# Decay attention and four experts on one core: the own terms of units 2 and 3 from a t-major product summed on VectorE

## The chip, the core and the metric

The kernel runs on one core of a Trainium2 chip. The metric is the device time of one execution in microseconds; the time before is the median of three runs, 913.03 us (912.9 to 913.32). Beside it stands one profiled execution, from which all durations below are read.

## The reference

Two parts follow each other. The first is a recurrence with a decaying state, for 4 batches, 8 heads, 768 steps and 48 dimensions per head; the second sends its output, as 3072 rows of 384 numbers, through 4 experts and weights them with `domain_probs`.

```python
for t in range(S):
    kt, vt, rt, wt = (k[:, :, t], v[:, :, t], r[:, :, t], w[:, :, t])
    cur = np.einsum('bhd,bhe->bhde', u[None] * kt, vt)
    y[:, :, t] = np.einsum('bhd,bhde->bhe', rt, state + cur)
    state = wt[:, :, :, None] * state + np.einsum('bhd,bhe->bhde', kt, vt)
...
p = domain_probs / (domain_probs.sum(-1, keepdims=True) + 1e-09)
for e in range(E):
    h = np.maximum(x @ w1[e], 0.0)
    out += p[:, e:e + 1] * (h @ w2[e])
```

The term with `cur` is what a step gives to itself: for each head it is the number `sum over d of r*u*k` times v. These numbers are called own terms here.

## The kernel before

The 768 steps are cut into 6 chunks of 128; a chunk of one batch is a unit, and there are 24: unit n is batch n % 4 of chunk n // 4. Units 0 to 3 are the first chunk. A unit goes through these helpers, all nested in `chunked_path`:

- `load` (L164) issues its transfers on SyncE's queue: `w` (tile wx), `k`, `r` with the head's dimension on the partitions (d-major), `v` with the step on the partitions (t-major), and `own`: r and k t-major in one tile `rkt` of 128x768, from a pool with one buffer.
- `after_decays` and `until_decays` (L237 to L259) make the products of decays on VectorE: the scan L241 to tile g, two tiny steps L251 and L252, the scan L253 to tile e. `scale` (L261) multiplies r by e (L263) and k by g (L264), in place, on VectorE.
- `own_product` and `diag_sum` (L184, L208) make the own terms, 8 per step, in tile dg (128x8). For chunk 0 POOL (VectorE for unit 0) multiplies r and k d-major (L192, 112x512), TensorE multiplies that with u in four products of 2 columns each (L215), and ScalarE copies the sums out of PSUM (L216). For all later chunks POOL multiplies r and k t-major and then u, which stands repeated in tile u_sb (L194, L195, 128x384 each), and VectorE sums over the dimensions (L218).
- `place` (L220) spreads dg over an identity, one half of the heads per call, to tile a0 or a1: either in four scaled copies on ScalarE (L227) or in one multiplication on POOL (L229). `DIAG` says which; for units 2 and 3 it is POOL for a0 and ScalarE for a1.
- `scores` (L266): TensorE multiplies scaled k and r (L272) and transposes k (L278). `masking` (L285) writes the scores below the diagonal into a0 and a1 on VectorE (L288). `values` (L290) multiplies a0 and a1 with v (L302, L306; ScalarE copies the result out, L308) and `carry` (L359) updates the state (L368).
- `guard` (L376) is a test of the decays on ScalarE (L379, L380).

The experts work on the output of a chunk. `f1` (L397) makes one of 8 slices of the hidden layer: TensorE (L405 for the first expert on chunk 0, otherwise L411), then ScalarE's relu to tile hh (L417) and VectorE's remainder to tile hl (L418); the product stands in one of three PSUM buffers, pf1, until both have read it. `f2` (L420) is the second layer (L431). The weights arrive as tiles `raw` and are split by `split_w` (L146) in two parts, with a cast on ScalarE (L151) and two subtractions on POOL (L156).

Everything is issued in an order written by hand from L558 on, and each engine works through its instructions in that order. While units 1 to 3 are made, the first expert's slices for batch 0 and batch 1 go in between: `begin(b, f)` is slice f for batch b, and `split_w2(q)` splits quarter q of the first expert's w2. A list `steps` holds the helpers of the units from unit 2's scores on; `go()` takes the next from it. For unit n they are `step_a` (after_decays of n+1, scores of n, own_product of n+1), `step_b` (until_decays of n+1), `step_c` (masking of n), `step_d` (scale, diag_sum and place of n+1, then the transfer `own` of unit n+2) and `step_e` (values and carry of n, and transfers). So unit 3's scale, diag_sum and place stand in `step_d(2)`, ahead of begin(1,5), and unit 2's values follow it.

```python
            begin(1, f)
            if f in (0, 1, 3, 4, 5):
                go()
            if f == 2:
                split_w2(2)
                guard(1)
                load(4, "w")
```

Of the kernel before, what the change touches and what calls it, by code (L numbers as in the profile page):

```python
# [39 lines left out]
SEG = (2, 2)  # L40
# [6 lines left out]
def chunked_path(ctx, tc, dmaj, tmaj, u_bc, probs, w1, w2, out, flag):  # L47
    nc = tc.nc
# [25 lines left out]
    u_sb = const.tile([128, DM], F32, name="u_sb")  # L74
# [20 lines left out]
    def setup_a():  # L95
        nc.gpsimd.memset(zero.bitcast(F32), 0.0)
        nc.gpsimd.memset(u_col, 0.0)
        nc.vector.memset(ones1, 0.0)
        nc.vector.memset(ones1[:, C + 1::C + 1], 1.0)
        nc.vector.memset(zst, 0.0)  # L100
        nc.gpsimd.memset(ident, 1.0)
        nc.gpsimd.affine_select(out=ident, in_=ident, compare_op=ALU.is_gt, fill=0.0, base=0,
                                pattern=[[1, C]], channel_multiplier=-1)
        nc.gpsimd.tensor_copy(mask, ident)
        make_identity(nc, ident)

    def act_table():
        nc.vector.memset(chk[:, 0:1], 0.0)
        nc.scalar.copy(chk[:, 1:2], chk[:, 0:1])
# [26 lines left out]
    def load_own(q):  # L136
        nc.sync.dma_start(out=w1_own[:, q], in_=w1[0, q])
# [26 lines left out]
    def load(n, what):  # L164
        if n >= NU:
            return
        s = un.setdefault(n, dict(c=n // B, b=n % B))
        if what == "w":
            s["wx"] = p_wx.tile([ROWS, WLEN], F32, name="wx", tag="wx")
            nc.sync.dma_start(out=s["wx"], in_=dmaj[n, :, 2 * NP * C:])  # L170
        elif what in ("r", "k"):
            x = p_in.tile([ROWS, NP, C], F32, name=what, tag=what)
            o = 0 if what == "r" else NP * C
            nc.sync.dma_start(out=x, in_=dmaj[n, :, o:o + NP * C].rearrange("p (i t) -> p i t", i=NP))
            s[2 * what] = x
        elif what == "own":
            t = p_one.tile([128, 2 * DM], F32, name="rkt", tag="rkt")
            nc.sync.dma_start(out=t, in_=tmaj[n, :, 0:2 * DM])
            s["rt"], s["kt"] = t[:, 0:DM], t[:, DM:2 * DM]
        else:  # L180
            s["v"] = p_in.tile([128, DM], F32, name="v", tag="v")
            nc.sync.dma_start(out=s["v"], in_=tmaj[n, :, 2 * DM:])

    def own_product(n):  # L184
        s = un[n]
        if s["c"] == 0:

            if not spare:
                spare.append(p_acc.tile([128, B, DM], F32, name="acc", tag="acc").rearrange("p b d -> p (b d)"))
            o = n % 2 * NP * C  # L190
            t = s["own"] = spare[0][0:ROWS, o:o + NP * C].rearrange("p (i t) -> p i t", i=NP)
            (nc.vector if n == 0 else nc.gpsimd).tensor_tensor(t, s["rr"], s["kk"], ALU.mult)  # L192
            return
        nc.gpsimd.tensor_tensor(s["rt"], s["rt"], s["kt"], ALU.mult)  # L194
        nc.gpsimd.tensor_tensor(s["rt"], s["rt"], u_sb, ALU.mult)  # L195

    def load_u():
        for j in range(2):
            nc.sync.dma_start(out=u_col[half(j), :, j],
                              in_=u_bc[0, :].rearrange("(i j d) -> j d i", j=2, d=D)[j],  # L200
                              allow_slow_non_contiguous=True)
# [6 lines left out]
    def diag_sum(n):  # L208
        s = un[n]
        dg = s["dg"] = p_two.tile([128, 2, NP], F32, name="dg", tag="dg")  # L210
        s["a"] = []
        if s["c"] == 0:
            p = ps_f2.tile([128, DM], F32, name="pf2", tag="pf2")[:, 0:2 * NP].rearrange("p (j i) -> p j i", j=2)
            for i in range(NP):
                nc.tensor.matmul(p[:, :, i], s["own"][:, i, :], u_col[:, i, :], start=True, stop=True)  # L215
            nc.scalar.copy(dg, p)  # L216
        else:
            nc.vector.tensor_reduce(dg, s["rt"].rearrange("p (i j d) -> p j i d", j=2, d=D), AX.X, ALU.add)  # L218
# [339 lines left out]
    with tc.manual_schedule():  # L558
        act_table()
        setup_a()  # L560
        for what in ("w", "k", "r"):
            load(0, what)
        load_u()
        load(0, "v")
        warm_up(FILL[0])
        for what in ("w", "k", "r"):
            load(1, what)
        load_own(0)
        load(1, "v")
        load_own(1)  # L570
        load(2, "w")
        load_own(2)
        setup_b()


        after_decays(0)
        own_product(0)
        own_score(0)
        until_decays(0)
        warm_up(FILL[1])  # L580
        scale(0)
        last_pair(0)
        own_product(1)
        after_decays(1)
        scores(0)
        for what in ("k", "r"):
            load(2, what)
        load_own(3)
        for q in range(2):
            more_raw()  # L590
        masking(0)
        last_pair(1)
        until_decays(1)
        values(0)
        diag_sum(1)
        carry(0)
        load(2, "v")
        place(1, 0)
        scale(1)

        def begin(b, f):
            f1(passes[0][1], 0, f, b * C, C, True)

        def split_w2(q):
            split_next((passes[0][1], 2, q), True)

        begin(0, 0)
        scores(1)
        for what in ("k", "r"):
            load(3, what)  # L610
        for q in range(2):
            more_raw()
        place(1, 1)
        after_decays(2)
        own_product(2)
        begin(0, 1)
        masking(1)
        begin(0, 2)
        guard(0)
        load(3, "w")  # L620
        split_w2(0)
        values(1)
        carry(1)
        load(3, "v")
        begin(0, 3)
        until_decays(2)
        begin(0, 4)
        begin(0, 5)
        scale(2)
        last_pair(2)  # L630
        diag_sum(2)
        begin(0, 6)
        split_w2(1)
        place(2, 0)
        place(2, 1)
        begin(0, 7)
        nc.sync.dma_start(out=u_sb, in_=u_bc)
        nc.sync.dma_start(out=pr, in_=probs)
        del steps[-2 * len(parts):]
        for f in range(FT):  # L640
# [7 lines that stand above are left out]
            if f == 4:  # L648
                last_pair(3)
            if f == 6:  # L650
                split_w2(3)
        script = {7: (go,), 8: (go,), 9: (setup_c, lambda: guard(2), lambda: load(5, "w"), go),
                  10: (go, lambda: guard(3), lambda: split_x(0)), 12: (lambda: split_x(1),), 13: (go,)}
        for pi, (g, e) in enumerate(passes):
            first, last = pi % NE == 0, pi % NE == NE - 1
            for blk in g:
                segs = SEG if pi == 0 else (B,)
                b0 = 0
                for nb in segs:
                    next_w1 = blk == g[-1] and pi + 1 in fresh and b0 + nb == B  # L660
                    own_w2 = blk == g[0] and pi in fresh and pi > 0
                    if pi == 0:
                        pace[:] = 0.2, 0.6
                    elif blk >= GROUPS[-1][0]:
                        pace[:] = 0.6, 1.0
                    else:
                        pace[:] = 0.4, 0.8

                    def work(i):
                        q = i % FT // 2  # L670
                        if own_w2 and i < FT and i % 2 == 0:
                            split_next((e, 2, q), True)
                        if next_w1 and i >= FT and i % 2 == 0:
                            split_next((passes[pi + 1][1], 1, q), True)
                        if i == FT - 1 and last and b0 + nb == B:
                            read.add(blk)
                        if pi == 0 and b0 == 0:
                            for f in script.get(i, ()):
                                f()
                            return True  # L680
                        if pi == 0 and i in (9, 11):
                            split_x(2 + (i - 9) // 2)

                    if first:
                        upto(blk * B + b0 + nb - 1)
                    turn(e, blk, first, last, b0, nb, pi == 0, pi == 0 and b0 == 0, work)
                    b0 += nb
# [189 lines left out]
```

## Time and profile before

| what | value |
|---|---|
| median of three runs | 913.03 us |
| the profiled execution | 913.18 us |
| its span, first to last instruction | 911.5 us |
| TensorE busy | 899.6 us, 99% |
| VectorE busy | 351.5 us, 39% |
| ScalarE busy | 257.8 us, 28% |
| POOL busy | 267.1 us, 29% |
| read from memory | 60.86 MB |

The execution's own time is longer than the span by what lies before the first and after the last instruction. PE is TensorE, DVE VectorE, ACT ScalarE, POOL GpSimd, and SP SyncE, which issues the transfers. An engine's busy time is a sum over the whole span; where it waits, and for whom, is told by the views that go by time.

### The profile page before, as it was taken

The page shows a single profiled execution, that of the slowest core. Times are in us where ns is not written, and L with a number is a line of the kernel's source. Part 1 is how long each engine was busy: PE and PEld are TensorE (multiplying, and loading weights), DVE is VectorE, ACT ScalarE, POOL GpSimd, SP SyncE. Part 2 cuts the span into 40 slices and gives each one's busy share as a digit, 9 for nine tenths or more (in the row PEclk, how much of TensorE's full clock was granted, in tenths as well). Part 3 has the DMA queues.
Part 4 walks back from the last instruction along what each step waited for, and adds up shares of the span by engine and source line. Part 5 has one row for each costly group of instructions (what it writes and reads, how often), then busy time and mean ns, then how long its engine had stood idle before and what let it go on. Part 6 is the DMA issues. An engine that isn't in the chain of part 4 may idle for free.

```text
span 911.5 us, 13796 instructions
## 1 busy us (share of the span) xinstructions
PE 899.6 (99%) x5675; PEld 810.2 (89%) x5675; DVE 351.5 (39%) x564; ACT 257.8 (28%) x482; POOL 267.1 (29%) x278
## 2 busy tenths in 40 slices
PE   8999999999999999999999999999999999999997
PEld 6898989898898988998989889899899899889987
DVE  6756555546363622122455642202222221221221
ACT  4555343322234132133221332232212310321110
POOL 3638766622255332033312220042003300230000
PEclk9999999999999999999999999999999999999999
DMA  9625435441334222111324210021002200110001
GB/s 249 196 65 180 158 119 170 137 129 56 93 105 147 67 70 68 35 58 65 105 72 131 75 49 29 1 79 61 1 1 70 69 1 1 35 35 36 18 18 38
DMA packets 36423, 70.48 MB, mean 77 GB/s; under 512 B 5376, under 2 KB 15488, under 8 KB 36352
## 3 DMA queue, kind: packets, MB, share of 16 engines
q1 hardware_dynamic: 36352, 69.53, 24.7%
q8 instruction: 46, 0.75, 0.4%
q14 instruction: 25, 0.20, 0.1%
HBM read 60.86 MB, written 4.72 MB: 72 GB/s over the span
## 4 chain that ended last, share of the span: by engine, by line
PE 98%; ACT 1%; DVE 1%; issue 0%; POOL 0%; DVEq 0%; ACTq 0%; POOLq 0%
PE pf L431 44%; PE pf L411 41%; PE sc L272 3%; PE yp L322 2%; PE pf L405 2%; PE yp L317 1%; PE kt L278 1%; PE up L368 1%; PE pf L115 1%; ACT a L227 0%; PE pf L215 0%; PE pf L302 0%; PE pf L306 0%; DVE zst L251 0%; ACT wx L380 0%; DVE a L288 0%
## 5 line engine op out<-in xcount | busy, mean ns | idle before, releaser
L411 PE MATMUL pf<-x,w1h 128*128 128x512 f32 x1104 | 342.0, 391 | 0.0
L431 PE MATMUL pf<-w2h,hh 128*128 128x384 f32 x768 | 259.7, 338 | 0.0
L431 PE MATMUL pf<-w2h,hl 128*128 128x384 f32 x768 | 257.2, 335 | 0.0
L431 PE MATMUL pf<-w2l,hh 128*128 128x384 f32 x768 | 256.9, 335 | 0.0
L418 DVE SCALAR_TENSOR_TENSOR hl<-pf,hh 128x512 fp32r<-128x512 f32 (+2 forms) x208 | 134.7, 649 | 285.0 <-ACT hh L417 284.3
L411 PEld LDWEIGHTS pf<-x,w1h 128*128 128x128 f32 x1104 | 205.8, 188 | 42.4 <-issue 0.4
L417 ACT ACTIVATE hh<-pf 128x512 fp32r<-128x512 f32 (+2 forms) x208 | 117.2, 565 | 428.1 <-PE pf L411 417.0
L411 PE MATMUL pf<-x,w1l 128*128 128x512 f32 x552 | 215.2, 390 | 0.0
L156 POOL TENSOR_TENSOR w1l<-raw,w1h 128x384 fp32r<-128x384 f32 x72 | 74.8, 1068 | 253.0 <-ACT w1h L151 253.0
L431 PEld LDWEIGHTS pf<-w2h,hh 128*128 128x128 f32 x768 | 144.2, 188 | 2.2 <-issue 0.4
L431 PEld LDWEIGHTS pf<-w2l,hh 128*128 128x128 f32 x768 | 144.2, 188 | 0.9
L431 PEld LDWEIGHTS pf<-w2h,hl 128*128 128x128 f32 x768 | 144.1, 188 | 0.0
L411 PEld LDWEIGHTS pf<-x,w1l 128*128 128x128 f32 x552 | 103.6, 188 | 21.7
L440 DVE SCALAR_TENSOR_TENSOR acc<-pf,pr,acc 128x384 f32<-128x384 f32 x72 | 44.5, 618 | 201.1 <-PE pf L431 201.1
L156 POOL TENSOR_TENSOR w2l<-raw,w2h 128x384 fp32r<-128x384 f32 x80 | 84.6, 1079 | 115.3 <-ACT w2h L151 104.5
L229 POOL TENSOR_TENSOR a<-ident,dg 128x512 f32<-128x512 f32 x42 | 44.7, 1084 | 125.9 <-DVE dg L218 121.9
L241 DVE TENSOR_TENSOR_SCAN g<-wx,ones 112x516 f32<-112x516 f32 x24 | 33.1, 1381 | 1.6 <-DMA wx<-in_dmaj 1.6
L151 ACT CAST w2h<-raw 128x768 fp32r<-128x768 f32 x40 | 33.0, 826 | 0.0
L328 ACT CAST y<-yp 112x256 fp32r<-112x256 f32 x20 | 7.5, 373 | 89.6 <-PE yp L322 88.6
L288 DVE COPY_PREDICATED a<-mask,sc 128x512 f32<-128x512 uint32 x48 | 32.2, 726 | 1.0 <-POOL a L229 0.7
L438 ACT ACTIVATE acc<-pf,pr 128x384 f32<-128x384 f32 x24 | 14.0, 581 | 64.4 <-PE pf L431 64.2
L253 DVE TENSOR_TENSOR_SCAN e<-wx,zst 112x516 f32<-112x516 f32 x24 | 31.8, 1324 | 0.8
(76 smaller groups left out, 495.1 us busy)
## 6 DMA issues: line engine op xcount, KB each, us to landing
raw<-in_w SPq DMA_DIRECT2D x76, 384.0 KB, 3.1
rkt<-in_tmaj SPq DMA_DIRECT2D x20, 384.0 KB, 3.1
wx<-in_dmaj SPq DMA_DIRECT2D x24, 226.2 KB, 3.1
k<-in_dmaj SPq DMA_DIRECT2D x24, 224.0 KB, 3.2
r<-in_dmaj SPq DMA_DIRECT2D x24, 224.0 KB, 3.4
v<-in_tmaj SPq DMA_DIRECT2D x24, 192.0 KB, 2.7
out<-acc SPq DMA_DIRECT2D x24, 192.0 KB, 1.9
x<-y SPq DMA_DIRECT2D x80, 48.0 KB, 2.2
```

The lines of the kernel that those rows point to most:

```text
L151: nc.scalar.copy(hi, t)
L156: eng.tensor_tensor(lo[:, s], t[:, s], hi[:, s].bitcast(F32), ALU.subtract)
L229: nc.gpsimd.tensor_tensor(a, ident.unsqueeze(1).to_broadcast([128, NP, C]), dg[:, q].unsqueeze(2).to_broadcast([128, NP, C]), ALU.mult)
L241: nc.vector.tensor_tensor_scan(g[:, WLEN - 1:0:-1], wx[:, WLEN - 1:0:-1], ones1[:, WLEN - 1:0:-1], 0.0, ALU.mult, ALU.add)
L253: nc.vector.tensor_tensor_scan(e, wx[:, 0:WLEN - 1], zst.rearrange("p i t -> p (i t)"), 0.0, ALU.mult, ALU.add)
L272: nc.tensor.matmul(sc[:, j, i, :], s["kk"][half(j), i, :], s["rr"][half(j), i, :], start=True, stop=True)
L288: nc.vector.copy_predicated(s["a"][j], mask.unsqueeze(1).to_broadcast([128, NP, C]), s["sc"][:, j])
L411: nc.tensor.matmul(p[:, 0:nt], wv[:, k, fs], x[:, k, bs, i, :], start=(k == 0 and n == 0), stop=(k == KT - 1 and n == 2))
L417: nc.scalar.activation(hh[:, ts], p[:, 0:nt], AF.Relu)
L418: nc.vector.scalar_tensor_tensor(hl[:, ts], p[:, 0:nt], 0.0, hh[:, ts].bitcast(F32), ALU.max, ALU.subtract)
L431: nc.tensor.matmul(p, hv[:, ts], wv[:, o, :], start=(f == 0 and n == 0), stop=(f == FT - 1 and n == 2))
L440: nc.vector.scalar_tensor_tensor(a[:, b, :], p, sc, a[:, b, :], ALU.mult, ALU.add)
```

## The change

`own_product` and `diag_sum` take the way over TensorE for units 0 and 1 alone (`SEG[0]` is 2). Units 2 and 3 now go the way of the later chunks: they need u_sb early and a transfer `own` each, and unit 2's product is issued later, after the split of w2's first quarter.

```diff
     def own_product(n):
         s = un[n]
-        if s["c"] == 0:
+        if n < SEG[0]:
...
         s["a"] = []
-        if s["c"] == 0:
+        if n < SEG[0]:
             p = ps_f2.tile([128, DM], F32, name="pf2", tag="pf2")[:, 0:2 * NP].rearrange("p (j i) -> p j i", j=2)
...
         load_own(3)
+        nc.sync.dma_start(out=u_sb, in_=u_bc)
+        load(2, "own")
         for q in range(2):
             more_raw()
...
         after_decays(2)
-        own_product(2)
         begin(0, 1)
...
         split_w2(0)
+        own_product(2)
         values(1)
...
         diag_sum(2)
+        load(3, "own")
         begin(0, 6)
...
         begin(0, 7)
-        nc.sync.dma_start(out=u_sb, in_=u_bc)
         nc.sync.dma_start(out=pr, in_=probs)
```

The order of the instructions shows what this moves. First SyncE's queue, from unit 2's k on (k, r, v and wx belong to the units in turn; raw is a quarter of w2 or w1, x the first expert's w1). Before:

```order
L174 DMA k_234<-in_dmaj 112x512
L174 DMA r_236<-in_dmaj 112x512
L137 DMA x_121<-in_w1 128x768
L143 DMA raw_239<-in_w2 128x768
L143 DMA raw_241<-in_w2 128x768
L182 DMA v_283<-in_tmaj 128x384
L174 DMA k_316<-in_dmaj 112x512
```

After the change:

```order
L174 DMA k_234<-in_dmaj 112x512
L174 DMA r_236<-in_dmaj 112x512
L137 DMA x_121<-in_w1 128x768
L589 DMA u_sb_105<-in_u_bc 128x384
L178 DMA rkt_240<-in_tmaj 128x768
L143 DMA raw_242<-in_w2 128x768
L143 DMA raw_244<-in_w2 128x768
L182 DMA v_286<-in_tmaj 128x384
L174 DMA k_319<-in_dmaj 112x512
```

u_sb and unit 2's rkt now stand ahead of the first two quarters of w2 and of unit 2's v and unit 3's k and r. Unit 3's rkt follows unit 3's v, further down.

Second, VectorE and ScalarE around unit 3's own terms (dg_525 before, dg_526 after; hh_401 and hl_402 before are those of begin(1,4), hh_409 and hl_410 those of begin(1,5); after the change they are hh_405, hl_406 and hh_413, hl_414). VectorE before:

```order
L251 TENSOR_SCALAR zst_104<-g_461 112x4
L252 RECIPROCAL zst_104<-zst_104 112x4
L253 SCALAR_TENSOR_TENSOR e_513<-wx_352,zst_104 112x516
L418 SCALAR_TENSOR_TENSOR hl_402<-pf1_517,hh_401 128x128
L263 TENSOR_TENSOR r_318<-r_318,e_513 112x512
L264 TENSOR_TENSOR k_316<-k_316,g_461 112x512
L418 SCALAR_TENSOR_TENSOR hl_410<-pf1_542,hh_409 128x128
```

VectorE after the change, with one row more:

```order
L251 TENSOR_SCALAR zst_104<-g_461 112x4
L252 RECIPROCAL zst_104<-zst_104 112x4
L253 SCALAR_TENSOR_TENSOR e_514<-wx_354,zst_104 112x516
L418 SCALAR_TENSOR_TENSOR hl_406<-pf1_518,hh_405 128x128
L263 TENSOR_TENSOR r_321<-r_321,e_514 112x512
L264 TENSOR_TENSOR k_319<-k_319,g_461 112x512
L218 TENSOR_REDUCE dg_526<-rkt_422 128x8
L418 SCALAR_TENSOR_TENSOR hl_414<-pf1_538,hh_413 128x128
```

ScalarE at the same place before, where the copy L216 takes unit 3's sums out of PSUM:

```order
L417 ACTIVATE hh_401<-pf1_517 128x128
L216 COPY dg_525<-pf2_526 128x8
L227 ACTIVATE a1_534<-ident_101,dg_525 128x128 x4
L417 ACTIVATE hh_409<-pf1_542 128x128
L308 COPY acc_264<-pf1_548 128x3x128
L371 COPY st2_110<-up_562 112x192
```

ScalarE after the change, without that copy:

```order
L417 ACTIVATE hh_405<-pf1_518 128x128
L227 ACTIVATE a1_530<-ident_101,dg_526 128x128 x4
L417 ACTIVATE hh_413<-pf1_538 128x128
L308 COPY acc_267<-pf1_544 128x3x128
L371 COPY st2_110<-up_558 112x192
```

The sum over the dimensions now stands on VectorE behind unit 3's scale, and the four scaled copies on ScalarE, with hh of begin(1,5) behind them, read its result. Unit 2 has the same pattern: its L218 stands behind its L264.

Third, TensorE from unit 2's last carry product on, through begin(1,6) (pf1_576, then pf1_572), begin(1,7) (pf1_589, then pf1_585) and unit 3's scores, with the engines whose semaphores each waits for. Before:

```order
L368 MATMUL up_562<-v_283,ks_477 48x48
L405 MATMUL pf1_576<-acc_264,x_121 128x128 [waits DVE_49]
L405 MATMUL pf1_576<-acc_264,x_121 128x128 x2
L405 MATMUL pf1_589<-acc_264,x_121 128x128 [waits Activation_49]
L405 MATMUL pf1_589<-acc_264,x_121 128x128 x2
L272 MATMUL sc_597<-r_318,k_316 128x128 [waits DVE_49]
```

After the change:

```order
L368 MATMUL up_558<-v_286,ks_477 48x48
L405 MATMUL pf1_572<-acc_267,x_121 128x128 [waits DVE_49]
L405 MATMUL pf1_572<-acc_267,x_121 128x128 x2
L405 MATMUL pf1_585<-acc_267,x_121 128x128 [waits DVE_49]
L405 MATMUL pf1_585<-acc_267,x_121 128x128 x2
L272 MATMUL sc_593<-r_321,k_319 128x128 x8
```

The buffer of begin(1,7) was freed by ScalarE's copy L308 of unit 2's values; now it is freed by hl of begin(1,5) on VectorE, which is behind k's scaling there, so that the scores have no wait of their own left.

## Rows read from the trace of the kernel before

**Rows 1.** The page, busy time of each engine, with share and instructions.

```profile
PE 899.6 (99%) x5675; PEld 810.2 (89%) x5675; DVE 351.5 (39%) x564; ACT 257.8 (28%) x482; POOL 267.1 (29%) x278
```

**Rows 2.** Who TensorE waited for: us in total, times, longest.

```profile
PE pf L302 <- DVE a L288: 2.1, 2, 1.7
```

**Rows 3.** TensorE in order of time: start, us, instruction, idle before and releaser.

```profile
25.01 0.95 PE L215 MATMUL pf<-u_col,acc 112*128 112x2 f32 x8
...
28.00 1.16 PE L272 MATMUL sc<-r,k 48*128 48x128 f32 x16
...
33.02 1.05 PE L215 MATMUL pf<-u_col,acc 112*128 112x2 f32 x8 [0.62 <-POOL acc L192]
...
37.63 1.60 PE L405 MATMUL pf<-acc,x 128*128 128x128 f32 x12 [0.88 <-DVE hl L418]
39.17 1.16 PE L272 MATMUL sc<-r,k 48*128 48x128 f32 x16
```

**Rows 4.** The chain that ended last, 18 to 46 us: start, us, what.

```profile
34.04 1.87 DVE zst L251
...
36.16 1.25 DVE e L253
...
37.44 0.15 DVE hl L418
```

**Rows 5.** Transfers: one issue; KB and us to landing of three; DMA share, 10 to 28 us.

```profile
12.24 0.91 SPq L143 DMA_DIRECT2D raw<-in_w  x2
...
raw<-in_w SPq DMA_DIRECT2D x1, 384.0 KB, 8.0
...
u_sb<-in_u_bc SPq DMA_DIRECT2D x1, 192.0 KB, 5.9
...
rkt<-in_tmaj SPq DMA_DIRECT2D x1, 384.0 KB, 4.0
...
10.00:28.00 18.00, 15.53 (x182) 13.95 (x178) 11.21 (x23) 10.41 (x32) 6.01 (x7) 1.00 1.05 277
```

In the last of these rows the columns are the stretch, its length, the busy time of PE, PEld, DVE, ACT and POOL, TensorE's granted clock, the share of the DMA engines and GB/s.

**Rows 6.** POOL in order of time.

```profile
21.88 1.96 POOL L156 TENSOR_TENSOR w2l<-raw,w2h 128x384 fp32r<-128x384 f32 x2 [2.12 <-ACT w2h L151]
...
27.85 1.96 POOL L156 TENSOR_TENSOR w2l<-raw,w2h 128x384 fp32r<-128x384 f32 x2 [3.77 <-DVE hl L418]
...
34.84 1.03 POOL L229 TENSOR_TENSOR a<-ident,dg 128x512 f32<-128x512 f32 x1
...
42.55 1.01 POOL L194 TENSOR_TENSOR rkt<-rkt 128x384 f32<-128x384 f32 x1
43.63 1.00 POOL L195 TENSOR_TENSOR rkt<-rkt,u_sb 128x384 f32<-128x384 f32 x1
```

**Rows 7.** VectorE in order of time.

```profile
24.39 0.16 DVE L251 TENSOR_SCALAR zst<-g 112x4 f32<-112x4 f32 x1
...
26.93 0.69 DVE L264 TENSOR_TENSOR k<-k,g 112x512 f32<-112x512 f32 x1
...
33.96 1.95 DVE L251 TENSOR_SCALAR zst<-g 112x4 f32<-112x4 f32 x1
...
37.31 0.27 DVE L418 SCALAR_TENSOR_TENSOR hl<-pf,hh 128x128 fp32r<-128x128 f32 x1
...
38.09 0.69 DVE L264 TENSOR_TENSOR k<-k,g 112x512 f32<-112x512 f32 x1
...
40.02 1.75 DVE L241 TENSOR_TENSOR_SCAN g<-wx,ones 112x516 f32<-112x516 f32 x1
...
52.69 0.55 DVE L218 TENSOR_REDUCE dg<-rkt 128x8 f32<-128x384 f32 x1
```

**Rows 8.** ScalarE in order of time.

```profile
20.99 0.81 ACT L151 CAST w2h<-raw 128x768 fp32r<-128x768 f32 x1
...
34.31 1.28 ACT L227 ACTIVATE a<-ident,dg 128x128 f32<-128x128 f32 x4
35.49 0.25 ACT L417 ACTIVATE hh<-pf 128x128 fp32r<-128x128 f32 x1
```

## The prediction

> **What bounds the kernel now.** I read the busy shares first. TensorE is busy for 899.6 us, 99% of the span, and no other engine reaches 40% [rows 1]. The profiled execution took 913.18 us, 1.7 us more than its span of 911.5 us, and 0.15 us more than the median of 913.03 us. I make the sum against 913.18 and take the 0.15 us off at the end. Differences of 0.2%, 1.8 us, are about what a measurement of this kernel can tell.
>
> Next I read where TensorE waits. Its waits lie in the first 38 us; the longest in a stretch is 1.7 us, for a masked score tile [rows 2]. In the stretch that the change touches it waits twice: 0.62 us ahead of unit 3's four small products, for POOL's product of r and k, and 0.88 us ahead of begin(1,6), for a VectorE result that frees a PSUM buffer [rows 3]. From then on it runs without a wait to the end, so whatever the first 40 us gain or lose arrives at the end unchanged: there is no later slack to give a loss back, and none to swallow it.
>
> Then the chain of waits up to 37.6 us: it runs through VectorE (a 1.87 us step at the tiny L251, the scan L253, one hl) and then to begin(1,6) [rows 4]. Unit 3's small products, at 33.02 us, are not on it: TensorE was ahead there and waited afterwards anyway.
>
> **The change, part by part.** *TensorE* loses two groups of four products, 0.95 and 1.05 us busy, and the wait of 0.62 us [rows 3]: 2.6 us at most. The first group stands ahead of scores(2), which began at 28.00 us but also needs k(2), and VectorE finished that at 26.93 + 0.69 = 27.62 us [rows 7]; 0.4 us at most can be won there. The second group is followed by a wait on the chain above: nothing. ScalarE's two small copies of dg go with them, off the chain: nothing.
>
> *The transfers.* u_sb (192 KB) and unit 2's r and k (384 KB) now stand ahead of w2's first quarter. The engines are full between 10 and 28 us (share 1.05, 277 GB/s) and transfers land in the order of issue [rows 5], so 590,000 bytes delay all behind them by 2.1 us. The first quarter was issued at 12.24 us and landed 8.0 us later, at 20.2 us; I put it at 22.4 us. ScalarE's cast began at 20.99 us and took 0.8 us [rows 8]: now 23.2 us. POOL's subtractions took 1.96 us [rows 6]: now 23.2 to 25.2 us, where they ran from 21.88 us.
>
> *Unit 2's product on POOL* follows: 1.01 and 1.00 us [rows 6], to about 27.3 us if nothing stops it. Two products of 112x512 leave POOL, the first of them before 20 us, where it delayed nothing. The new ones fall where VectorE does L251 (24.39 us, 0.16 us), the scan and the two multiplications of scale(2), up to 27.62 us [rows 7]; POOL was idle from its copy before 24.1 us to 27.85 us [rows 6]. The two engines do not run such work side by side: L251 took 1.95 us at 33.96 us while POOL was busy, and the scan at 40.02 us took 1.75 us [rows 7] instead of 1.25 [rows 4]. So each POOL operation in this stretch pushes VectorE by its own length: 0.8 us that is left of the subtractions, 2.0 of products, less some 0.4 us of hl operations, which read PSUM and run beside: k(2) is ready at 27.6 + 2.4 = 30.0 us and scores(2) begins there, 2.0 us late. Bounds: 0.4 us gained if POOL always yields, 4 us lost if the second quarter's subtractions (1.96 us) get in as well.
>
> *Unit 2's reduction* (0.55 us, as unit 4's [rows 7]) comes after k(2), and ScalarE's four copies a1 of unit 2 (1.28 us, as unit 3's [rows 8]) wait for it, with the hh of begin(0,7) and begin(1,0) behind them on that engine. I carry 0.2 us for this, between 0 and 0.8 (0.55 + 0.28): L251 of unit 3, at 33.96 us before, starts at 36.2 us.
>
> *Unit 3's r and k* share one buffer with unit 2's, so their transfer is issued after that reduction, at about 30.6 us; such a one took 4.0 us [rows 5]. POOL's product then runs from 34.6 to 36.6 us, and the third quarter's subtractions behind it: POOL is again busy when L251 comes. I therefore keep the wait that it had, 1.95 - 0.16 = 1.8 us, and with it the 4.82 us from L251 to the end of k(3) (33.96 to 38.09 + 0.69 [rows 7]): k(3) is ready at 41.0 us. Bounds: 1.8 us less if there is no wait, 2 us more if the subtractions get in twice. Behind this transfer in SP's queue stand w1's first quarter, probs, k(4) and others; none is used before 42 us, so they cost nothing; if that cover fails, a transfer's 4 us is the price.
>
> *The order around unit 3's diagonal* is the largest term. TensorE made dg(3) without VectorE. Now the reduction stands behind scale(3) on VectorE, ScalarE's a1 of unit 3 waits for it, hh of begin(1,5) stands behind a1, hl of begin(1,5) behind that, and begin(1,7) waits for this hl to get its PSUM buffer, where before it waited for ScalarE's copy L308. From k(3): 0.55 (reduction) + 1.2 (a1) + 0.25 (hh) + 0.27 (hl) [rows 7, 8] + 0.1 of hand-overs = 2.4 us. Before, begin(1,7) started half-way between 37.63 and 39.17 us, at 38.4 us [rows 3], 0.4 us ahead of the end of k(3). The step costs 2.8 us, and 43.4 us is where begin(1,7) starts.
>
> The sum: 2.0 + 0.2 + 0 + 2.8 = 5.0 us, on 913.18 us: 918.2 us, or **918.0 us** against the median. The bounds added up: -0.4 + 0 - 1.8 + 2.8 = +0.6 us and 4 + 0.8 + 2 + 2.8 = +9.6 us.
>
> [...]
>
> **Rivals.** *Faster: VectorE, POOL and ScalarE have room.* All three parts of TensorE's 2.6 us would come out: 910.4 us. For it: these engines are 28 to 39% busy over the whole span. Against it: the share is an average, and the chain up to 37.6 us lies on VectorE, the engine that gets the reduction. It decides from the point at which hl of begin(1,5) is ready before 38.4 us, and for that k(3) would have to end at 36.0 us, 2.8 us before it does now. 4%. *No net change*: the waits fall by 1.8 us at L251 and by 0.4 us at scores(2), and begin(1,7) finds its buffer earlier than I think: within 1.8 us of 913. 4%. *The order alone*: the transfers are hidden, POOL yields, and only the last step costs: +2.8 us, 915.8 us, between 914.8 and 916.4 us. For it: the scan at 40.02 us lost only 0.5 us to POOL. Against it: L251 at 33.96 us lost 1.8 us. 17%. *Worse: TensorE also slows down.* [...] 14%. [...] That the change does not do what it says I exclude: the order of the instructions shows the two groups gone and the reductions in place.
>
> **How the numbers follow.** My own case, 916.4 to 920 us, has 61%, the two slower or milder neighbours 17% and 14%, and 8% lie at no change or faster. The range runs from 915.2 to 921.0 us: it leaves out the two small cases, half of the milder one's lower end and the upper end of the worse one, about 2 in 10. Faster 4%, the same 4%, slower 92%.
>
> **What would show it.** In the profile afterwards: w2's first quarter lands near 22.4 us; scores(2) starts near 30 us; L251 or the scan of unit 2 takes more than 1.5 times its free length; ScalarE's a1 of unit 3 waits for VectorE's L218; and TensorE has one new wait of 2 us or more ahead of begin(1,7), put down to hl L418, with a second one before scores(2). From there on every start is later by the same amount, with no new wait. I am wrong if begin(1,7) starts before 39 us, if TensorE has no wait over 1 us after 24 us, or if the loss sits later than 45 us.

## The result, and the profile after

The changed kernel took **920.4 us** (median of 4 runs, 919.56 to 920.94) against 913.17 us of the kernel before on the same chip: a ratio of 1.0075, 95% interval 1.0063 to 1.0088. The profiled execution took 919.56 us, 6.38 us more than the profiled one of before. In 5 of the 14 profiled executions below TensorE's clock also falls for a while between 13 and 26 us (to 0.50 in run 7), whatever the kernel; those of before and after don't have it, and where an experiment has it, it has a star in the table and I count from scores(2) on.

The page's busy line, and TensorE's waits for hl (total, times, longest). They answer to [rows 1] and [rows 2]:

```profile
PE 900.6 (98%) x5659; PEld 810.4 (88%) x5659; DVE 354.2 (39%) x566; ACT 257.1 (28%) x480; POOL 269.4 (29%) x280
```
```profile
PE pf L405 <- DVE hl L418: 5.7, 4, 2.5
```

TensorE's busy time grew by 1.0 us although eight products (16 instructions) left it. The wait for POOL's product [rows 3] is gone; the waits for hl are 5.7 us, where 0.88 stood before [rows 3], and scores(2) waits 1.2 us for k. TensorE's timeline (start, length, line, operation, [wait ahead of it]), against [rows 3]:

```profile
23.04 2.94 PE L405 MATMUL pf<-acc,x 128*128 128x128 f32 x24
...
30.54 1.16 PE L272 MATMUL sc<-r,k 48*128 48x128 f32 x16 [1.23 <-DVE k L264]
...
39.74 0.94 PE L405 MATMUL pf<-acc,x 128*128 128x128 f32 x6 [0.93 <-DVE hl L418]
43.20 0.94 PE L405 MATMUL pf<-acc,x 128*128 128x128 f32 x6 [2.52 <-DVE hl L418]
44.07 1.75 PE L272 MATMUL sc<-r,k 48*128 48x128 f32 x16
...
64.22 1.16 PE L272 MATMUL sc<-r,k 48*128 48x128 f32 x16
```

The row at 23.04 us opens with begin(0,3), that at 64.22 us is scores(4). scores(2) begins at 30.54 us (28.00 before) and begin(1,7), after a wait of 2.52 us, at 43.20 us (38.40). Then comes something that the sum did not have: the 16 small products of scores(3) take 1.75 us, where those of scores(2) took 1.16. The windows of this stretch say why (length; busy of TensorE, weight loads, VectorE, ScalarE, POOL; granted clock; DMA share; GB/s):

```profile
40.00:44.00 4.00, 1.48 (x12) 1.23 (x11) 1.93 (x5) 2.61 (x9) 1.29 (x2) 1.00 0.42 116
44.00:48.00 4.00, 4.00 (x27) 3.71 (x26) 3.45 (x6) 1.66 (x5) 3.62 (x3) 0.57 0.65 199
48.00:50.00 2.00, 2.00 (x14) 2.00 (x13) 1.90 (x5) 0.79 (x2) 1.76 (x3) 1.00 0.44 126
```

From 44 to 48 us the granted clock is 0.57: it is 0.50 from 44.5 to 47.5 us. From 48 us on it is 1.00 again. In the kernel before it is 1.00 all through 38 to 64 us.

begin(0,3) and scores(4) of the kernel before:

```profile
22.90 2.27 PE L405 MATMUL pf<-acc,x 128*128 128x128 f32 x18
...
57.74 1.16 PE L272 MATMUL sc<-r,k 48*128 48x128 f32 x16
```

scores(4) starts at 64.22 us, 57.74 before, and behind that point the times agree: 855.3 us remain in the one and 855.4 in the other. So the 6.5 us split into four stretches: 0.1 up to begin(0,3), 2.4 to scores(2) (7.50 instead of 5.10 us), 2.3 to begin(1,7) (12.66 instead of 10.40), 1.7 to scores(4) (21.02 instead of 19.34).

The engines behind it, VectorE against [rows 7] and POOL against [rows 6]:

```profile
24.53 0.81 DVE L251 TENSOR_SCALAR zst<-g 112x4 f32<-112x4 f32 x1
25.59 1.88 DVE L253 TENSOR_TENSOR_SCAN e<-wx,zst 112x516 f32<-112x516 f32 x1
27.77 1.31 DVE L263 TENSOR_TENSOR r<-r,e 112x512 f32<-112x512 f32 x1
29.00 1.48 DVE L264 TENSOR_TENSOR k<-k,g 112x512 f32<-112x512 f32 x1
...
36.63 0.85 DVE L251 TENSOR_SCALAR zst<-g 112x4 f32<-112x4 f32 x1
...
40.21 0.68 DVE L264 TENSOR_TENSOR k<-k,g 112x512 f32<-112x512 f32 x1
40.81 0.54 DVE L218 TENSOR_REDUCE dg<-rkt 128x8 f32<-128x384 f32 x1
42.85 0.29 DVE L418 SCALAR_TENSOR_TENSOR hl<-pf,hh 128x128 fp32r<-128x128 f32 x1 [1.50 <-ACT hh L417]
```
```profile
22.40 1.95 POOL L156 TENSOR_TENSOR w2l<-raw,w2h 128x384 fp32r<-128x384 f32 x2 [10.52 <-ACT w2h L151]
24.30 1.00 POOL L194 TENSOR_TENSOR rkt<-rkt 128x384 f32<-128x384 f32 x1
25.39 0.99 POOL L195 TENSOR_TENSOR rkt<-rkt,u_sb 128x384 f32<-128x384 f32 x1
...
27.53 2.40 POOL L156 TENSOR_TENSOR w2l<-raw,w2h 128x384 fp32r<-128x384 f32 x2
...
36.46 1.96 POOL L156 TENSOR_TENSOR w2l<-raw,w2h 128x384 fp32r<-128x384 f32 x2
```

L251 of unit 2 began at 24.53 us and ended at 25.34, when POOL's L194 (24.30 + 1.00) ended; the scan (1.88 instead of 1.23 us) stood beside L195; the two multiplications (1.31 and 1.48 instead of 0.68 and 0.69) beside the second quarter's subtractions. In the other half, dg (40.81) follows k(3), and hl (42.85) waits 1.50 us for ScalarE, which is here, against [rows 8]:

```profile
21.49 0.83 ACT L151 CAST w2h<-raw 128x768 fp32r<-128x768 f32 x1 [0.27 <-DMA raw<-in_w]
...
41.39 1.28 ACT L227 ACTIVATE a<-ident,dg 128x128 f32<-128x128 f32 x4 [4.82 <-DVE dg L218]
42.57 0.26 ACT L417 ACTIVATE hh<-pf 128x128 fp32r<-128x128 f32 x1
```

### The profile page after: what moved, and what is told of

Read it like the earlier page. It is cut to its first block, busy times and chain, and to the rows that moved or that the text cites. A ratio compares the mean times of both kernels' runs of the same rounds, so it can differ in the third digit from the quotient of the medians.

```text
span 917.8 us, 13766 instructions
## 1 busy us (share of the span) xinstructions
PE 900.6 (98%) x5659; PEld 810.4 (88%) x5659; DVE 354.2 (39%) x566; ACT 257.1 (28%) x480; POOL 269.4 (29%) x280
## 4 chain that ended last, share of the span: by engine, by line
PE 96%; DVE 2%; ACT 1%; issue 1%; DMA 0%; SPq 0%; DVEq 0%; ACTq 0%
PE pf L431 44%; PE pf L411 41%; PE sc L272 3%; PE yp L322 2%; PE pf L405 2%; PE yp L317 1%; PE kt L278 1%; PE up L368 1%; DMA r<-in_dmaj 0%; DVE k L264 0%; PE pf L302 0%; ACT a L227 0%; PE pf L306 0%; DVE r L263 0%; DVE zst L251 0%
## 5 line engine op out<-in xcount | busy, mean ns | idle before, releaser
L229 POOL TENSOR_TENSOR a<-ident,dg 128x512 f32<-128x512 f32 x42 | 43.8, 1063 | 130.9 <-DVE dg L218 126.9
```

What stands on the lines that cost most here:

```text
L229: nc.gpsimd.tensor_tensor(a, ident.unsqueeze(1).to_broadcast([128, NP, C]), dg[:, q].unsqueeze(2).to_broadcast([128, NP, C]), ALU.mult)
```

## The experiments

Four theories were to be told apart: **turns** (POOL and VectorE don't do such work side by side, and unit 2's products on POOL make k(2) late); **transfers** (w2's first quarter lands late, and that is the loss); **order** (hh and hl of begin(1,5) stand behind unit 3's reduction and a1); **clock** (the stand before begin(1,7), that is TensorE's wait of 2.52 us there, lets the clock fall, and that costs on its own). The table has each profiled execution: the stretch from begin(0,3) to scores(2), the start of begin(1,7), the stretch from scores(2) to scores(4), and times; a star marks those that lost 0.5 us or more to the clock before scores(2). Where begin(1,6) and begin(1,7) stand in one row, the start of the second is taken half-way.

| kernel | to scores(2) | begin(1,7) | scores(2) to scores(4) | profiled | median of runs |
|---|---|---|---|---|---|
| before | 5.10 | 38.40 | 29.74 | 913.18 | 913.2 to 913.3 |
| after | 7.50 | 43.20 | 33.68 | 919.56 | 920.40 |
| 1 hh first | 7.38 | 40.80 | 30.96 | 916.57 | 916.65 |
| 2 filler | 5.74 | 41.41 | 32.17 | 916.70 | 917.56 |
| 3 unit 2 alone | 7.12 | 39.17 | 28.71 | 914.15 | 914.25 |
| 4 unit 3 alone | 5.46 | 40.75 | 34.89 | 918.70 | 918.73 |
| 5 product first | 4.95 | 40.33 | 35.08 | 918.72 | 919.42 |
| 6 raws first * | 5.67 | 41.94 | 35.15 | 920.07 | 920.07 |
| 7 before, early loads * | 5.11 | 43.73 | 29.74 | 918.81 | 913.82 |
| 8 product first, filler * | 5.63 | 41.77 | 31.81 | 916.47 | 916.79 |
| 9 reordered | 4.91 | 36.93 | 30.20 | 913.30 | 913.88 |
| 10 masks first * | 5.44 | 38.71 | 30.02 | 914.74 | 913.96 |
| 11 and w2 late | 4.91 | 37.74 | 29.06 | 913.65 | 913.82 |
| 12 before, w2 late * | 5.68 | 38.80 | 28.78 | 913.40 | 912.35 |

**1. hh of begin(1,5) ahead of unit 3's diagonal.** Order.

```diff
         if n + 1 < NU:
             scale(n + 1)
+            if n == 2:
+                return
             own_score(n + 1)
...
             begin(1, f)
+            if f == 5:
+                own_score(3)
+                load(4, "own")
```

> The changed kernel with unit 3's reduction and its two diagonals issued behind begin(1,5), so that hh and hl of begin(1,5) no longer stand behind the reduction and a1. My theory (order): begin(1,7) waits only for hl of begin(1,5), which now follows the end of k(3) at 40.9 us: 40.9 + 0.3 + 0.1 = 41.3 us instead of 43.2, the stand shrinks from 2.5 to 0.6 us, the granted clock stays at 1.00 behind it, and values(3) starts near 47 instead of 50.4 us: 3.5 us less than the changed kernel, about 3 us more than before. Rival (begin(1,7) is held by something other than a1, such as k(3) itself or the late transfer of unit 3): it stays near 43.2 us and the time stays within 1 us of the changed kernel.

Median 916.65 us, ratio 1.004 (1.0027 to 1.0054). TensorE's row:

```profile
40.80 0.94 PE L405 MATMUL pf<-acc,x 128*128 128x128 f32 x6 [1.14 <-DVE hl L418]
```

begin(1,7) came 2.4 us earlier than in the changed kernel, the stand shrank to 1.14 us, the clock stayed at 1.00; in all 3.0 us were won in the profiled execution and 3.75 us on the medians. Order holds for this part, and the rival falls. Of the clock's 1.7 us behind begin(1,7) only 0.65 were won (20.37 us to scores(4), 21.02 in the changed kernel and 19.34 before): TensorE has new waits in this stretch, 0.32 us for ScalarE ahead of its transposes (L278) and 0.18 for a mask among them.

**2. TensorE kept busy through the stand.** Clock.

```diff
             if f == 6:
                 split_w2(3)
+                p = ps_f2.tile([128, DM], F32, name="pf2", tag="pf2")
+                for i in range(14):
+                    nc.tensor.matmul(p, zero[:, 0:128], zero[:, 0:DM], start=True, stop=True)
```

> The changed kernel with 14 products of zeros (128x384) on TensorE between begin(1,6) and begin(1,7); the result doesn't use them. My theory (clock): TensorE is busy through the stand, the granted clock stays at 1.00 from 40 to 48 us, begin(1,7) starts at 43.2 to 43.5 us, scores(3) takes 1.2 us as in the kernel before instead of 1.75, and values(3) starts near 49.0 us: 1.2 to 1.6 us less than the changed kernel. Rival (the slow stretch behind begin(1,7) comes from operands that other engines hand over late): values(3) stays at 50.4 us, the time doesn't change.

Median 917.56 us, ratio 1.0044 (1.0031 to 1.0058):

```profile
38.08 2.69 PE L656 MATMUL pf<-zero 128*128 128x384 f32 x14
41.41 0.94 PE L405 MATMUL pf<-acc,x 128*128 128x128 f32 x6 [0.65 <-DVE hl L418]
42.28 1.16 PE L272 MATMUL sc<-r,k 48*128 48x128 f32 x16
```

scores(3) took 1.16 us, and from begin(1,7) to scores(4) 19.42 us passed, 19.34 before and 21.02 in the changed kernel: 1.6 us, as the clock theory says. The start of begin(1,7) did not come as expected: 41.41 instead of 43.2 us, since L251 of unit 2 began at 24.41 us, ahead of L194 (24.46), and took 0.16 us. The same instructions took turns in another sequence, and k(2) was ready 1.9 us earlier. So the gain of 2.9 us is the clock's only in part; run 8 separates the two.

**3 and 4. Unit 2 alone, unit 3 alone.**

```diff
-        if n < SEG[0]:
+        if n < SEG[0] or n == 3:
...
-        load(3, "own")
```
```diff
-        if n < SEG[0]:
+        if n <= SEG[0]:
...
-        nc.sync.dma_start(out=u_sb, in_=u_bc)
-        load(2, "own")
...
         diag_sum(2)
+        nc.sync.dma_start(out=u_sb, in_=u_bc)
         load(3, "own")
```

> The changed kernel with unit 3 done as before (products on TensorE, its scaled product on POOL), unit 2 alone on the new way, u_sb and unit 2's r and k still loaded early. My theory: scores(2) starts at 30.5 us as in the changed kernel; k(3) ends some 2 us later than before, at 40.9 us; begin(1,7) starts 0.4 us ahead of that as it did before, at 40.5 us; no stand above 1.5 us, clock at 1.00; 2 us more than before. Rival (the early transfers and what they delay are the whole loss): 6 to 7 us more than before, as the changed kernel. Rival (unit 2 costs nothing that arrives at the end): within 0.5 us of before.

> The changed kernel with unit 2 done as before and unit 3 alone on the new way; u_sb is loaded just ahead of unit 3's r and k, so nothing new stands ahead of w2's first quarter. My theory: scores(2) starts at 28.0 us as before, k(3) ends near 38.8 us, begin(1,7) starts 2.4 us later at 41.2 us, after a stand of 1.5 to 2.5 us; the clock then costs 0 to 1.6 us: 2.8 to 4.4 us more than before. Together with the run of unit 2 alone the two extras make that of the changed kernel, 6.4 to 7.2 us. Rival (the order around unit 3's diagonal is hidden once nothing before it is late): within 1 us of before.

Unit 2 alone: median 914.25 us, ratio 1.0006 (0.9997 to 1.0015). Unit 3 alone: 918.73 us, ratio 1.0062 (1.0048 to 1.0075). TensorE's rows of the first and of the second, and the second's windows:

```profile
29.80 1.16 PE L272 MATMUL sc<-r,k 48*128 48x128 f32 x16 [1.22 <-DVE k L264]
...
38.40 1.60 PE L405 MATMUL pf<-acc,x 128*128 128x128 f32 x12
```
```profile
40.75 1.22 PE L405 MATMUL pf<-acc,x 128*128 128x128 f32 x6 [2.52 <-DVE hl L418]
41.90 2.08 PE L272 MATMUL sc<-r,k 48*128 48x128 f32 x16
```
```profile
40.00:44.00 4.00, 3.25 (x23) 2.81 (x24) 2.27 (x4) 2.13 (x7) 2.40 (x4) 0.66 0.91 302
44.00:48.00 4.00, 4.00 (x15) 4.00 (x16) 3.75 (x10) 1.97 (x4) 3.29 (x4) 0.50 0.26 61
```

With unit 2 alone scores(2) was 1.8 us late (29.80 us, 30.5 expected), but only 0.8 us of that were left at begin(1,7): L251 of unit 3 took 0.20 us there instead of 1.95. I had expected 2 us more than before and got 1.0. With unit 3 alone unit 2's product is made as before, but on POOL it keeps its new place behind `split_w2(0)` (23.86 us, 18.50 before), and L251 of unit 2 took 0.70 us beside it; scores(2) was nearly on time (28.41 us), begin(1,7) came 2.3 us behind the end of k(3) (38.44 us), and then the clock was low for longer than in the changed kernel (0.66 from 40 to 44 us and 0.50 to 48 us, where that had 1.00 and 0.57): scores(3) took 2.08 us, and 22.55 us passed to scores(4), 3.2 us more than before. It cost 5.5 us in the profiled execution where I allowed 4.4. Together the extras of the profiled executions are 6.5 us, within the 6.4 to 7.2 expected, but that is luck, since each size missed: L251's wait is not fixed, and the clock cost 3.2 us here and 1.7 in the changed kernel.

**5. Unit 2's products on POOL ahead of the subtractions.** Turns against transfers.

```diff
-        split_w2(0)
         own_product(2)
+        split_w2(0)
```

> The changed kernel with unit 2's two products put on POOL ahead of the subtractions of w2's first quarter, where POOL idles until 22.4 us; the transfers stand as in the changed kernel. My theory (POOL and VectorE take turns): the products run from 19.1 us, when unit 2's r and k land, to 21.2 us, and VectorE's L251, scan and two multiplications of unit 2 meet at most the tail of the subtractions: k(2) ends at 27.7 to 28.4 us instead of 30.5, scores(2) starts there. Unit 3's order is left as it is, so begin(1,7) follows the end of k(3) by 2.3 us, at about 41 us after a stand of 2.5 us, and the clock falls as in the changed kernel or as in the run of unit 3 alone: 917 to 918.7 us, 1 to 3 us less than the changed kernel. Rival (unit 2 is late because w2's first quarter lands late): scores(2) stays at 30 us or later, the time does not change.

Median 919.42 us, ratio 1.0069 (1.0055 to 1.0083). VectorE's rows, TensorE's, and the windows:

```profile
24.36 0.20 DVE L251 TENSOR_SCALAR zst<-g 112x4 f32<-112x4 f32 x1
24.81 1.23 DVE L253 TENSOR_TENSOR_SCAN e<-wx,zst 112x516 f32<-112x516 f32 x1
...
27.54 0.55 DVE L218 TENSOR_REDUCE dg<-rkt 128x8 f32<-128x384 f32 x1
```
```profile
27.82 1.16 PE L272 MATMUL sc<-r,k 48*128 48x128 f32 x16
...
40.33 1.54 PE L405 MATMUL pf<-acc,x 128*128 128x128 f32 x6 [3.08 <-DVE hl L418]
41.80 2.08 PE L272 MATMUL sc<-r,k 48*128 48x128 f32 x16
```
```profile
40.00:44.00 4.00, 3.67 (x23) 3.22 (x24) 2.00 (x5) 1.71 (x5) 2.49 (x2) 0.56 0.79 271
44.00:48.00 4.00, 4.00 (x17) 4.00 (x17) 3.83 (x9) 1.97 (x4) 2.89 (x4) 0.59 0.28 66
```

L251 and the scan are back at 0.20 and 1.23 us, and scores(2) starts at 27.82 us, although the subtractions ran later than in the changed kernel (22.58 us). That decides for turns, against transfers. Of the 2.9 us won at begin(1,7) 1.3 were left at scores(4) and 0.8 in the time: the stand was 3.08 us and the clock cost 3.2 us (22.57 us to scores(4)). The median missed my range by 0.7 us.

**6. w2's quarters ahead of u_sb and of unit 2's r and k**. Turns against transfers once more.

```diff
-        nc.sync.dma_start(out=u_sb, in_=u_bc)
-        load(2, "own")
         for q in range(2):
             more_raw()
+        nc.sync.dma_start(out=u_sb, in_=u_bc)
+        load(2, "own")
         masking(0)
```

> The changed kernel with the loads of w2's first two quarters issued ahead of u_sb and of unit 2's r and k, so that these quarters land as in the kernel before. My theory (turns): the subtractions run from 21.9 us as before, the two products follow at 23.9 to 25.9 us and still meet L251 and the scan: scores(2) starts at 29.3 to 30.3 us, at most 1 us earlier than in the changed kernel, and the time is 0 to 1.5 us less. Rival (late transfers): scores(2) starts at 28.0 to 28.4 us, 2 us or more are won.

Median 920.07 us, ratio 1.0072 (1.0058 to 1.0085). Inconclusive: the profiled execution lost some 1.5 us to the clock at 20 to 26 us (begin(0,3) started 0.8 us late, and the 24 products from there took 3.69 us instead of 2.94), VectorE's L251 therefore began only at 25.89 us, when POOL's products were over, and met none of them. That no time was won fits turns, but the clock's 3.2 us (22.56 us from begin(1,7) to scores(4)) hide what the earlier scores(2) brought.

**7. The kernel before with the early loads.** Transfers.

```diff
         load_own(3)
+        nc.sync.dma_start(out=u_sb, in_=u_bc)
+        load(2, "own")
...
         begin(0, 7)
-        nc.sync.dma_start(out=u_sb, in_=u_bc)
```

> The kernel before with u_sb and unit 2's r and k (which it doesn't use) loaded where the changed kernel loads them, and nothing else changed: the delay of the transfers by itself. My theory: w2's first quarter lands 1 us later, the subtractions run at 22.4 to 24.4 us and touch L251 of unit 2 for 0.4 us at most; scores(2) starts at 28.0 to 28.5 us and the time is 0 to 0.7 us above before. Rival (the transfers are the loss of unit 2): scores(2) starts at 30 us, 2 us or more above before.

Median of 12 runs 913.82 us, ratio 1.0007 (0.9998 to 1.0016). The profiled execution is the highest of them: its clock was at half (0.50) for most of 14 to 23 us, and begin(0,3) started 5.3 us late. From there on it keeps the times of before to 0.01 us:

```profile
12.00:16.00 4.00, 3.48 (x27) 2.91 (x27) 3.62 (x7) 0.48 (x1) 0.00 (x0) 0.65 1.04 253
16.00:20.00 4.00, 4.00 (x30) 3.67 (x32) 0.00 (x0) 1.74 (x7) 1.28 (x1) 0.50 1.02 381
```
```profile
28.23 2.27 PE L405 MATMUL pf<-acc,x 128*128 128x128 f32 x18
...
33.34 1.16 PE L272 MATMUL sc<-r,k 48*128 48x128 f32 x16
```

28.23 to 33.34 us is 5.11, before 22.90 to 28.00; scores(2) to scores(4) is 29.74 in both. The shift in that execution covers the delay of the quarter, so it is the ratio over all the runs (the other 11 took 913.01 to 915.30 us) that speaks: the loads by themselves cost some 0.6 us, at most 1.5 by the upper end of the interval, and not the rival's 2 us or more.

**8. Runs 5 and 2 together.** Clock, without the other sequence of turns.

> The kernel with unit 2's products first, and with the 14 products of zeros between begin(1,6) and begin(1,7) as well; the result doesn't use them. Without them that kernel took 918.72 us in its profiled execution: begin(1,7) was only 1.93 us later than before, but the granted clock was 0.50 to 0.67 from 41 to 48 us. My theory (the stand of 3.08 us lets the clock fall, and that costs 3.6 us): begin(1,7) stays at 40.3 to 40.7 us, the clock at 1.00, the time is 915 to 915.7 us, 3 us or more below. Rival (the slow products come from late operands or from something else in this stretch): 918 us or more.

Median 916.79 us, ratio 1.0033 (1.002 to 1.0046), 2.6 us below run 5. This profiled execution lost 1.5 us at 22 to 26 us, so its begin(1,7) is later; from there:

```profile
41.77 0.94 PE L405 MATMUL pf<-acc,x 128*128 128x128 f32 x6 [0.63 <-DVE hl L418]
42.63 1.16 PE L272 MATMUL sc<-r,k 48*128 48x128 f32 x16
```
```profile
40.00:44.00 4.00, 3.37 (x32) 2.81 (x31) 1.50 (x4) 3.05 (x10) 2.34 (x4) 1.00 0.75 230
44.00:48.00 4.00, 4.00 (x32) 3.75 (x32) 3.90 (x8) 1.97 (x4) 3.92 (x4) 1.00 0.56 166
```

19.42 us to scores(4), 22.57 without the products of zeros: 3.15 us, with the same instructions on the other engines. The clock theory is shown. The time missed its range by 1.1 us (915 to 915.7 expected); a loss of 1.5 us like that of the profiled execution would account for it, but the four other runs have no trace.

**9 to 11. Both orders mended**: run 5's swap, begin(1,5) ahead of scale(3), and unit 3's reduction and diagonals behind carry(2); then, in 10, unit 3's masked copies ahead of unit 4's scan; then, in 11, `split_w2(2)` behind these.

```diff
-            if f in (0, 1, 3, 4, 5):
+            if f in (0, 1, 3):
+                go()
+            if f == 5:
+                go()
                 go()
+                own_score(3)
+                load(4, "own")
```

> The changed kernel with both orders mended: unit 2's products ahead of the first subtractions, begin(1,5) ahead of scale(3), and unit 3's reduction and diagonals behind values(2) and carry(2). My theory: scores(2) starts near 28.0 us; begin(1,7) waits for no diagonal, its hl stands ahead of k(3), so scores(3) starts when k(3) ends, at 37 to 39.5 us (before: 39.2); the clock stays at 1.00; the four small products that TensorE lost are won in part: 911.5 to 914 us. Rival (the new work on VectorE and POOL makes k(3) late in any order): scores(3) starts at 41 us or later, 915 us or more.

```diff
     def step_a(n):
-        if n + 1 < NU:
+        if n + 1 < NU and n != 3:
             after_decays(n + 1)
...
     def step_c(n):
         masking(n)
+        if n == 3:
+            after_decays(n + 1)
```

> The reordered kernel with unit 3's two masked copies put ahead of unit 4's scan on VectorE. In the reordered kernel scores(3) ran 1.1 us earlier than before, and values(3) then waited for the masks (0.60 and 0.26 us, carry ended at 45.98 us where 44.9 was possible). My theory: the masks end by 41.5 us, values(3) follows the 18th product of f2 at 42.9 us without a wait, 1.1 us is won: 912.0 to 912.6 us. Rival (the wait moves to the next user of unit 4's scan): 913 us or more.

> The same, with the split of w2's third quarter moved behind scale(3), so that POOL's subtractions (33.8 to 36.7 us) no longer stand beside the scan and the two multiplications of unit 3. My theory (POOL and VectorE take turns): the scan takes 1.25 instead of 1.74 us, the multiplications 0.7 each instead of 1.04 and 0.80, k(3) ends at 37.2 instead of 37.9 us and scores(3) follows: 0.5 to 0.9 us less than the kernel with the masks first, 911.2 to 912.0 us. Rival (the quarter then lands too late for f2, or the subtractions meet the reduction and the masks): no gain or a loss.

Medians 913.88, 913.96 and 913.82 us; ratios 1.0007 (0.9998 to 1.0016), 1.0006 (0.9997 to 1.0014) and 0.9997 (0.9988 to 1.0005). In the first scores(3) started at 38.04 us, 1.1 us ahead of before, and values(3) then waited for its masks:

```profile
38.04 1.16 PE L272 MATMUL sc<-r,k 48*128 48x128 f32 x16 [0.28 <-DVE k L264]
...
43.51 0.43 PE L302 MATMUL pf<-a,vz 128*64 128x128 f32 x2 [0.60 <-DVE a L288]
```

Run 9 came out at the upper end of its range. Putting the masks first took this wait away, and a wait of 0.66 us for hl came at 56.5 us instead: 0.2 us were won from scores(2) to scores(4), none on the median, so the rival of that run holds. Run 11 is 0.2 us shorter than before up to scores(2) and 0.7 from there to scores(4), but no faster on the median, and not by the 0.5 to 0.9 us expected; its profiled execution began 1.0 us late, since a scan at 9.29 us, right behind the start of a product on POOL (9.28), took 2.35 us instead of 1.23. Four of its 12 runs (912.08 to 912.75 us) lie below the lowest of before's 29 (912.84), so the order can gain, but run 12's best are as low (911.94) without the change. With both orders mended the change comes out even with before, and its 2.6 us are still not won: where products of TensorE left, it now waits for hl (0.22, 0.49 and 0.56 us in run 11 between scores(2) and scores(4)), so VectorE's chain sets the pace.

**12. The kernel before with `split_w2(2)` behind carry(2)**, and nothing of the change.

```diff
             if f == 2:
-                split_w2(2)
                 guard(1)
...
+            if f == 5:
+                split_w2(2)
```

> The kernel before with that same move alone: the split of w2's third quarter behind values(2) and carry(2). My theory: L251 of unit 3 no longer waits for POOL (0.16 to 0.4 us instead of 1.95), k(3) ends at 37.2 to 37.8 us instead of 38.78, the wait of 0.88 us ahead of begin(1,6) goes: 912.2 to 912.6 us, 0.6 to 1 us less than before, without any of the change. Rival (something else holds begin(1,6)): 913 us.

Median 912.35 us, ratio 0.9986 (0.9975 to 0.9997), the lowest of all and 0.9 us below before. VectorE's row and TensorE's:

```profile
34.74 0.15 DVE L251 TENSOR_SCALAR zst<-g 112x4 f32<-112x4 f32 x1
```
```profile
38.03 1.60 PE L405 MATMUL pf<-acc,x 128*128 128x128 f32 x12
```

L251 takes 0.15 us, the wait of 0.88 us ahead of begin(1,6) [rows 3] is gone, and scores(2) to scores(4) is 1.0 us shorter.

## Why the prediction held, and where it was off

The range (915.2 to 921.0) held the 920.4 us, and the sign was right. The forecast of 918.0 was 2.4 us low, though: 920.4 us lies outside my own case (916.4 to 920) and inside the band of the rival *Worse* (920 to 922 us, which no row of before showed). Step by step, in the profiled executions:

- *TensorE's own 2.6 us.* Taken as 0.4 at most at scores(2) and nothing behind. It holds: even with both orders mended (runs 9 to 11) nothing clear of the noise arrived.
- *The transfers.* Mis-sized, without effect. I put w2's first quarter at 22.4 us, 2.2 us later than before; it was issued at 13.34 us and landed 8.1 us after that, at 21.4 us, 1.2 us later than before. ScalarE's cast, which waited for it, began at 21.49 us, 0.5 us later than before. Run 7 puts the cost of the loads alone at some 0.6 us.
- *POOL's product of unit 2: 2.0 us at scores(2).* Measured 2.4, and run 5 shows that it is the products' place, not the transfers. The mechanism held, but the size came out of other parts than those of the sum: L251 and the scan lost 0.65 us each beside the products, the 0.8 us for the first quarter's subtractions was not lost, and the two multiplications lost 1.4 us together beside the second quarter's subtractions (27.53 us), which I had only in the bound of 4 us. That hl runs beside POOL, 0.4 us of the sum, held: two of them took 0.46 us at 27.39 us with POOL busy, as long as before at 25.95 us with POOL idle.
- *0.2 us carried to L251 of unit 3.* Forecast at 36.2 us, found at 36.63.
- *L251 keeps its wait of 1.8 us.* This step failed. L251 of unit 3 took 0.85 us in the changed kernel, and 0.15 to 0.95 in every experiment but run 7, which keeps the order of before and has 1.96 again. The scan behind it took 1.77 us, though, so that k(3) came 4.26 us after the start of L251 and not 4.82: 0.6 us too much in the sum. Here the wait ended with the POOL instruction under way: L251 ended at 37.48 us, the subtraction at 37.46 (36.46 + 1.00). That L251 loses twice, as in before's row, where it ended at 35.91 us and POOL's L229 at 35.87 [rows 6, 7], holds for that one sequence.
- *The order: 2.8 us, begin(1,7) at 43.4 us.* Measured 2.3 us from the end of k(3) to begin(1,7), 2.4 forecast, and begin(1,7) at 43.20 us; run 1 takes it away, run 4 has it by itself.
- *The clock.* Left out of the sum and given to a rival with 14%; it is the larger part of the 2.4 us. By the sum begin(1,6) starts 2.2 us later than before, at 39.8 us, its products take 0.94 us, and begin(1,7) starts at 43.4 us: a stand of 2.7 us. The stand was 2.52 us, the granted clock fell from 1.00 to 0.50, and the stretch behind took 1.7 us more in the profiled execution. The three other runs were 0.5 to 1.4 us longer at lower mean clocks (0.993 to 0.994, 0.997 in the profiled one), which a longer fall would explain; they have no trace, so this stays open. No row of before shows the clock fall or what that costs; the rows after the change do: 1.00 up to 44 us, 0.57 from 44 to 48 us, and 1.75 us instead of 1.16 for the 16 products of scores(3). Run 8 puts 3.15 us on keeping TensorE busy through its stand.

Of the signs that I named, scores(2), the longer L251 and scan of unit 2, the reduction ahead of a1, and both new waits came as said. w2's first quarter came earlier, and "every start is later by the same amount" failed: begin(1,7) was 4.8 us later than before, scores(4) 6.5. Some 1.0 us of that came behind 45 us (unit 3's transposes L278 were 5.5 us later, 45.75 us instead of 40.26), which I had named as a sign of being wrong.

So up to 43.2 us the sum was right to 0.2 us, by errors that cancel: 0.4 too little up to L251 of unit 3, 0.6 too much behind it. That is luck, and so is part of the range's success. I was wrong to let the worse rival stand apart from my own case: the stand was in my sum, and its price belonged there with it.

## What to carry to other kernels

A wait that a change puts on TensorE is to be priced twice: its own length, and the slow products behind it, here 1.7 to 3.2 us for a stand of 2.5 to 3.1 us, and nothing on the clock for one of 1.14 us (run 1). Work that is moved from TensorE to engines with low busy shares costs what it delays on the chain that feeds TensorE: look at what stands behind it in each engine's queue, and beside it on the engine that it takes turns with (L251 and the scan of unit 2 took 0.81 and 1.88 us beside POOL's products, 0.20 and 1.23 us without them in run 5). Before taking work away, look for a wait on that chain that moving one line removes: run 12's median lies 0.9 us below before, and that of the change did not in any order tried.

## What was not expected of the hardware

- Stands of the same length cost differently: 2.52 us cost 1.7 us in the changed kernel and 3.2 us in run 4, 3.08 us cost 3.2 in runs 5 and 6. In the changed kernel begin(1,7) still ran at full length (0.94 us) and scores(3) was the first slow stretch; in run 4 begin(1,7) itself took 1.22 us. What decides the moment was not tried.
- The clock can fall without a stand of that length: in run 12's profiled execution, for one, TensorE was busy for 2.14 us of the 4 us from 18 to 22 us, with a longest wait of 1.65 us, and the clock was 0.87 from 20 to 22 and 0.50 from 22 to 24 us; before was busy for 2.14 us of the same 4 us, had the same wait, and kept 1.00. In run 7's it was at half for some 9 us. Why one execution falls and another does not stays open.
- VectorE and POOL's turns hang on less than 0.3 us: L251 began at 24.53 us, 0.23 us behind L194, and waited for it (0.81 us); at 24.41 us, 0.05 ahead of it, it took 0.16 us (run 2), and scores(2) came 1.9 us earlier. The reduction took no turn in run 5: 0.55 us at 27.54 us, in the middle of subtractions that began at 26.93 us and took 2.52.
